# Attention, routing and experts on one core: embedding, gates, ranks and early plan in steps of one slot, the early plan from two batches

## Chip, cores and metric

One core of a Trainium2 chip runs the whole program. The metric is the time of one execution in microseconds (us), the median of three runs for the kernel before. Engines are named as in the profile: PE (TensorE; PEld its weight loads), DVE (VectorE), ACT (ScalarE), POOL (GpSimd) and SP (SyncE, which here issues nearly all loads).

## What is computed

```python
# attention: q, k, v of (4 batches, 12 heads, 448 tokens, 64)
scores = matmul(q, k.T) / sqrt(64) - log(448)
attn_out = matmul(1 / (1 + exp(-scores)), v)
x = attn_out.transpose(0, 2, 1, 3).reshape(1792, 768)

# mixture of 8 experts, one expert per token
xn = x / (norm(x) + 1e-06);  en = emb / (norm(emb) + 1e-06)
logits = xn @ en.T / tau
expert_idx = argmax(logits, axis=1)
gate_w = softmax(logits)[arange, expert_idx]
out[mask_e] = gate_w * (relu(x[mask_e] @ w1[e]) @ w2[e])

# dense layer
h = out @ w_in              # (768, 2048)
y = (h - tanh(h)) @ w_out   # (2048, 768)
```

Every float32 product is made of three products of rounded parts (a high part h, a low part l: hh, hl, lh), so that each operand needs a cast (`w0h`, `vh`, `ah`) and a subtraction (`w0l`, `vl`, `al`).

## The kernel before

**Attention** runs from 0 to about 232 us. Its work is cut into 84 slots; 24 pairs of heads (6 for each of 4 batches) share them, 7 slots for two pairs. In slot u PE makes the scores of slot u (`pq`, line 233), then the products with v of slot u-3 (`pav`, line 256; LAG = 3). Between the two, ACT takes two sigmoids of `pq` (lines 240, 241) and DVE their difference `al` (line 242), which frees the PSUM tile of `pq`. When a pair is done, its columns are copied out (`xT`), and two slots later PE turns them into rows of tokens and logits (`pr`, line 281), which DVE adds to `u` (291) and copies into `rec` (292). For the pairs to come DVE casts `w0h`/`w1h` (199) and `vh` (210), and POOL makes `w0l`/`w1l` (202) and `vl` (211).

The PSUM tiles `pq`, `pr` and `prank` come from one tag, "qk", with three buffers in turn: a tile waits until the tile three allocations earlier has been read. Only PE's order is written out by hand: a loop over slots calls `scores(u)`, `av(u - LAG)` and `events(u)`, which runs what `plan(u, ...)` put down for that slot. The orders of DVE, ACT, POOL and SP are a scheduler's; each of these queues is worked off in that order.

**Routing.** When the last pair of a batch has its rows, `route` finds each token's expert (`route_a`) and plans the rest for fixed slots: the squares for the norm on ACT (`square`), the gate value (`gate`), the ranks of the tokens within their expert (`route_b`: `prank` on PE, then some ten small DVE operations that read it in PSUM, up to the row numbers `idx`) and four scatters of the rows to a table in DRAM, sorted by expert (`send_rows`, POOL, line 491, `x_tok`).

```python
if b == B - 2:
    plan(now[0] + ROUTE_E - 1, self.gate, b, r)      # ROUTE_E = 3
    plan(now[0] + ROUTE_E, self.route_b, b, r, pr)
    plan(now[0] + ROUTE_E, self.send_rows, b, r)
    plan(now[0] + ROUTE_E, self.early_rows)
    plan(ns, self.early_gates)
elif b < B - 1:
    plan(now[0] + ROUTE - 1, self.gate, b, r)        # ROUTE = 8
```

**Early plan.** After the third batch `early_rows` (called B - 2 = 2) chooses, from three batches' counts, the two expert groups of 256 tokens that are worked first (`plan_early`, some 60 small DVE operations named `pe_...`, up to the row numbers `gidx`), loads the first three quarters of the first group's w1 (`w1raw`, SP) and gathers both groups' rows (`gather_x`, POOL, line 698, `xg`). `early_gates` multiplies the first group's rows by their gates on ACT (line 706). So the experts can start at 239 us, while the last batch is routed. **Experts** run to about 560 us (9 groups, PE without pauses), the **dense layer** from there to the end.

Of the kernel before, what the change touches and what calls it, by code (L numbers as in the profile page):

```python
# [23 lines left out]
ROUTE, ROUTE_E = 8, 3  # L24
# [14 lines left out]
class Prog:  # L39
# [56 lines left out]
    def embedding(self):  # L96
        nc, E, NJ = self.nc, self.E, self.NJ
        cp, ep = self.cp, self.ep
        et = cp.tile([P, NJ, E], F32, name="emb_t")
        nc.sync.dma_start(et, self.emb)  # L100
        sq = ep.tile([P, NJ, E], F32, name="emb_sq")
        nc.vector.tensor_tensor(sq, et, et, ALU.mult)
        pt = self.ps1.tile([P, 2, 512], F32, tag="qk", name="emb_ss")[:, 0]
# [4 lines left out]
        self.norm_plus_eps(ss, sc[:, 0], sc[:, 1], self.mhalf[:, 0:1].to_broadcast([P, E]))  # L108
        nc.vector.reciprocal(sc[:, 0], sc[:, 1])
        self.ien = ep.tile([P, NJ, P + E], F32, name="ien")  # L110
        nc.vector.tensor_copy(self.ien[:, :, :P], self.ident.unsqueeze(1).to_broadcast([P, NJ, P]))
        nc.vector.tensor_tensor(
            self.ien[:, :, P:], et, sc[:, 0].unsqueeze(1).to_broadcast([P, NJ, E]), ALU.mult
        )

    def norm_plus_eps(self, ss, tmp, res, mhalf):

        nc = self.nc
        shape = list(ss.shape)
        r0 = self.sm.tile(shape, F32, tag="nr0", name="nr0")  # L120
        nc.vector.tensor_scalar(ss, ss, 1e-30, None, ALU.max)
        nc.gpsimd.tensor_tensor(r0, ss, mhalf, ALU.pow)
        nc.vector.tensor_tensor(tmp, r0, r0, ALU.mult)
        nc.vector.scalar_tensor_tensor(tmp, tmp, -0.5, ss, ALU.mult, ALU.mult)
        nc.vector.scalar_tensor_tensor(tmp, tmp, 1.5, r0, ALU.add, ALU.mult)
        nc.vector.tensor_tensor(tmp, tmp, ss, ALU.mult)
        nc.vector.tensor_scalar(res, tmp, 1e-6, None, ALU.add)


    def attention(self):  # L130
# [206 lines left out]
        with tc.manual_schedule(engines=pe):  # L337
# [10 lines left out]

            def route(i):
                b = pairs[i][0]  # L350
                bt = self.bts.pop(b)
                for c in range(NCH):
                    plan(now[0] + 1 + c // 2 if b < B - 1 else now[0], square, bt, c)
                r = self.route_a(bt)
                pr = lambda: ps1.tile([P, 2, 512], F32, tag="qk", name="prank")
                if b == B - 2:
                    plan(now[0] + ROUTE_E - 1, self.gate, b, r)
                    plan(now[0] + ROUTE_E, self.route_b, b, r, pr)
                    plan(now[0] + ROUTE_E, self.send_rows, b, r)
                    plan(now[0] + ROUTE_E, self.early_rows)  # L360
                    plan(ns, self.early_gates)
                    plan(ns + 1, self.early_columns, lambda: ps2.tile([P, 2, 512], F32, tag="qk", name="xt"))
                elif b < B - 1:
                    plan(now[0] + ROUTE - 1, self.gate, b, r)
                    plan(now[0] + ROUTE, self.route_b, b, r, pr)
                    plan(now[0] + ROUTE, self.send_rows, b, r)
                else:
                    self.last_route = b, r
# [11 lines left out]
            plan(5, self.embedding)  # L380
            now = [0]
            u = 0
            while u < ns + LAG:
                now[0] = u
                if u < ns:
                    scores(u)
                if LAG <= u < ns + LAG:
                    av(u - LAG)
                events(u)
                if u >= CONV:  # L390
                    conv()
                if u == ns and self.cv is not None:
                    for _ in self.cv:
                        pass
                u += 1
        while at:
            now[0] = u
            events(u)
            u += 1
        cx.close()  # L400

    def route_a(self, bt):
# [8 lines left out]
        nc.vector.tensor_reduce(mx, lg, AX.X, ALU.max)  # L411
        ls = sm.tile(A3, F32, tag="ls", name="ls")
# [9 lines left out]
        return bt, oh, ls  # L422

    def route_b(self, b, st, pst):
        bt, oh, ls = st
# [18 lines left out]
        V.tensor_tensor(o, o, cnt, ALU.subtract)  # L444
        rk = sm.tile(A3, F32, tag="rk", name="rk")
# [7 lines left out]
        bt["idx"] = idx  # L453

    def send_rows(self, b, st):

        bt = st[0]
# [9 lines left out]
    def gate(self, b, st):  # L467

        bt, oh, ls = st
        nc, sm = self.nc, self.sm  # L470
# [16 lines left out]
        nc.vector.reciprocal(bt["rec"][:, :, DM + 1 : DM + 2], gs.unsqueeze(2))  # L487

# [33 lines left out]
    def plan_early(self):  # L522
# [4 lines left out]
        cnt0 = self.n_before[:, self.B - 1]  # L527
        pls = []
        self.start = self.n_first = None
        for k in range(2):  # L530
# [11 lines left out]
            V.tensor_scalar(e, cm, -1.0, float(E), ALU.mult, ALU.add)  # L542
            m = t("m", P, 2)
# [9 lines left out]
            nb = self.B - 1  # L553
# [4 lines left out]
            V.tensor_reduce(vs, pr, AX.X, ALU.add)  # L558
            gidx = cp.tile([P, 1, 2], I32, name=f"gidx0{k}")
# [3 lines left out]
            V.tensor_copy(pl["e"], e)  # L563
            st = t("start", P, E)
# [9 lines left out]
            pls.append(pl)  # L574

# [7 lines left out]
        return pls  # L583
# [90 lines left out]
    def early_rows(self):  # L674
        self.pl0, self.pl1 = self.plan_early()
# [4 lines left out]
        nt = (self.B - 1) * self.S  # L680
        for s in (self.s0, self.s1):
            for h in range(2):
                self.gather_x(s, h, nt)
# [74 lines left out]
    def experts(self, cx):  # L758
# [83 lines left out]
        def last_route():  # L842
            self.route_b(*self.last_route, pst)
            self.gate(*self.last_route)
            self.send_rows(*self.last_route)
            pl.update(self.plan())
# [324 lines left out]
```

## Time and profile before

| | |
|---|---|
| median of 3 runs | 1052.88 us (1050.65 to 1053.71) |
| the profiled execution | 1052.65 us, its span 1050.9 us |
| PE busy, DVE busy | 97% and 79% of the span |
| 98.53 to 116.94 us, slots 35 to 41 | 18.41 us |
| 134.61 to 153.78 us, slots 49 to 55 | 19.17 us |
| 153.78 to 172.19 us, slots 56 to 62 | 18.41 us |
| 189.86 to 211.23 us, slots 70 to 76 | 21.37 us |
| 211.23 to 228.30 us, slots 77 to 82 | 17.07 us |

How to read it: a timeline row gives start, length, engine, line, operation and, in brackets, how long the engine stood idle before it and what released it. PE is in front of everything here, so a loss shows as a bracket on a PE row, or as a stretch of seven slots that is longer than a quiet one. What the other engines do counts where PE waits for it. All slot numbers count from 0.

### The profile page before, as it was taken

How to read it: one execution, taken by the hardware profiler on the slowest of the kernel's cores; microseconds unless marked ns; L12 is line 12 of the kernel's file. 1: busy time of each engine (PE TensorE's matmuls, PEld its weight loads, DVE VectorE, ACT ScalarE, POOL GpSimd, SP SyncE). 2: the span in 40 equal slices, each digit the busy share in tenths (PEclk: the TensorE clock that was granted, in tenths of full speed). 3: DMA queues.
4: the chain of work that ended last, by engine and by line, in shares of the span. 5: the costliest groups of instructions: out<-in, count | busy, mean ns of one | idle time of the engine just before them, and what ended most of it. 6: DMA issues, size and time to landing. Idle time of an engine off the chain costs nothing.

```text
span 1050.9 us, 16813 instructions
## 1 busy us (share of the span) xinstructions
PE 1016.5 (97%) x6437; PEld 939.6 (89%) x6437; DVE 828.9 (79%) x1172; ACT 557.0 (53%) x694; POOL 166.4 (16%) x178
## 2 busy tenths in 40 slices
PE   7999999899999999999998999999999999999997
PEld 5777777678999999999997899999999999999997
DVE  7879797978968878889963798888987676766774
ACT  6778787777666666666643544442453322332230
POOL 7345546342021001010000000000000300000002
PEclk9999999999999999999999999999999999999999
DMA  5422424338878984874922535454443522332212
GB/s 160 140 83 82 134 65 142 118 115 299 297 243 299 337 290 162 282 257 161 309 103 94 197 139 175 180 210 150 181 151 120 193 94 89 120 120 98 113 61 106
DMA packets 83527, 175.28 MB, mean 167 GB/s; under 512 B 7639, under 2 KB 62958, under 8 KB 83438
## 3 DMA queue, kind: packets, MB, share of 16 engines
q1 hardware_dynamic: 79598, 155.78, 43.2%
q0 software_dynamic: 3840, 18.35, 4.9%
q8 instruction: 52, 0.85, 0.3%
q14 instruction: 37, 0.30, 0.1%
HBM read 156.68 MB, written 36.30 MB: 184 GB/s over the span
## 4 chain that ended last, share of the span: by engine, by line
issue 57%; PE 29%; DVE 8%; POOL 3%; DMA 2%; ACT 1%; SPq 0%; POOLq 0%; DVEq 0%; ACTq 0%
PE pty L786 8%; PE pth L786 8%; PE pav L256 6%; PE pq L233 4%; POOL out_dram L491 2%; DVE al L242 2%; PE pr L281 1%; DVE vh L210 1%; DMA xg<-x_tok,gidx 1%; DVE wl L777 1%; PE xt L725 1%; DMA cr<-in_moe_w_in_dram 1%; ACT wh L776 1%; POOL vl L211 0%; DVE xT L271 0%
## 5 line engine op out<-in xcount | busy, mean ns | idle before, releaser
L1041 PE MATMUL o<-wo,gh 128*128 128x384 f32 x896 | 240.8, 335 | 0.7 <-DVE acc L1054 0.7
L1001 PE MATMUL z<-yh,wi 128*128 128x448 f32 x768 | 221.2, 370 | 4.1 <-ACT yh L973 3.8
L1041 PEld LDWEIGHTS o<-wo,gh 128*128 128x128 f32 x896 | 163.3, 188 | 2.3 <-DVE acc L1054 1.0
L1001 PEld LDWEIGHTS z<-yh,wi 128*128 128x128 f32 x768 | 144.3, 189 | 16.9 <-ACT yh L973 4.2
L1041 PE MATMUL o<-wo,gl 128*128 128x384 f32 x448 | 150.1, 335 | 0.1
L1001 PE MATMUL z<-yl,wi 128*128 128x448 f32 x384 | 138.0, 367 | 0.0
L786 PE MATMUL pth<-wi,wh 128*128 128x256 f32 x432 | 121.4, 282 | 2.9 <-ACT wi L729 1.2
L1054 DVE TENSOR_TENSOR acc<-o,acc 128x768 f32<-128x768 f32 x97 | 92.4, 952 | 39.5 <-PE o L1041 38.3
L786 PE MATMUL pty<-hh,wl 128*128 128x256 f32 x432 | 121.7, 284 | 0.2 <-DVE wl L777 0.2
L786 PE MATMUL pth<-wi,wl 128*128 128x256 f32 x432 | 121.3, 281 | 0.3 <-DVE wl L777 0.3
L786 PE MATMUL pty<-hh,wh 128*128 128x256 f32 x432 | 121.5, 285 | 0.0
L786 PE MATMUL pty<-hl,wh 128*128 128x256 f32 x432 | 121.3, 283 | 0.0
L786 PE MATMUL pth<-xl,wh 128*128 128x256 f32 x432 | 120.9, 280 | 0.0
L240 ACT ACTIVATE ah<-pq,bias_s 128x896 fp32r<-128x896 f32 x84 | 85.2, 1014 | 45.5 <-PE pq L233 45.5
L242 DVE TENSOR_TENSOR al<-pq,ah 128x896 fp32r<-128x896 f32 x84 | 90.4, 1084 | 23.8 <-ACT pq L241 23.3
L491 POOL DMA_INDIRECT out_dram<-acc,toki x14 | 17.2, 1232 | 577.9 <-DVE acc L1054 576.7
L1024 ACT CAST gh<-r 128x896 fp32r<-128x896 f32 x32 | 30.0, 938 | 135.1 <-DVE r L1022 82.2
L1008 ACT ACTIVATE t<-z 128x896 f32<-128x896 f32 x32 | 29.4, 920 | 127.3 <-PE z L1001 73.8
L777 DVE TENSOR_TENSOR wl<-w1raw,wh 128x768 fp32r<-128x768 f32 x72 | 68.2, 955 | 25.0 <-ACT wh L776 24.3
L1041 PEld LDWEIGHTS o<-wo,gl 128*128 128x128 f32 x448 | 84.1, 188 | 1.7 <-DVE gl L1025 0.4
L786 PEld LDWEIGHTS pth<-wi,wh 128*128 128x128 f32 x432 | 81.6, 189 | 3.5 <-ACT wi L729 1.4
L786 PEld LDWEIGHTS pty<-hh,wl 128*128 128x128 f32 x432 | 82.4, 191 | 0.4 <-DVE wl L777 0.4
(249 smaller groups left out, 2200.4 us busy)
## 6 DMA issues: line engine op xcount, KB each, us to landing
w1raw<-in_moe_w_dram SPq DMA_DIRECT2D x36, 768.0 KB
w2raw<-in_moe_w_dram SPq DMA_DIRECT2D x27, 1024.0 KB
wi<-dwi SPq DMA_DIRECT2D x32, 768.0 KB
wo<-dwo SPq DMA_DIRECT2D x32, 768.0 KB
cr<-in_moe_w_in_dram SPq DMA_DIRECT2D x16, 768.0 KB
dwi<-cr SPq DMA_DIRECT2D x16, 768.0 KB
cr<-in_moe_w_out_dram SPq DMA_DIRECT2D x16, 768.0 KB
dwo<-cr SPq DMA_DIRECT2D x16, 768.0 KB
```

What stands on the lines that cost most here:

```text
L233: nc.tensor.matmul(pq[:, x, :S], w[kt][p, c : c + P], w[qt][p, KW:], start=(m == 0), stop=(m == 2))
L240: nc.scalar.activation(hi, pv, AF.Sigmoid, **sc)
L242: nc.vector.tensor_tensor(lo, pv, f32(hi), ALU.subtract)
L256: nc.tensor.matmul(pav[:, :S], vo(vv), aa[:, x], start=(b0 and m == 0), stop=(e and m == 2))
L491: i = self.nc.gpsimd.indirect_dma_start(**kw)
L777: nc.vector.tensor_tensor(wl, cols, f32(wh), ALU.subtract)
L786: nc.tensor.matmul(pt[:, u], a[:, kk], b[:, kk], start=(n == 0), stop=(n == 3 * K - 1))
L1001: nc.tensor.matmul(z[:, g, :GT], wi[:, a, j * P : (j + 1) * P], b[:, j], start=(n == 0), stop=(n == 3 * NJ - 1),)
L1008: nc.scalar.activation(t, zv, AF.Square)
L1024: nc.scalar.copy(gv, r)
L1041: nc.tensor.matmul(o[:, w, :NW], a[:, u, i * P : (i + 1) * P], wo[:, b, w * NW : (w + 1) * NW], start=(n == 0), stop=(n == 3 * CH - 1),)
L1054: nc.vector.tensor_tensor(acc[i], ov, acc[i], ALU.add)
```

## The change

`embedding`, `route_a`, `norm_plus_eps`, `gate`, `route_b`, `early_rows` and `plan_early` become generators; a list of them is stepped once in each slot, after `events(u)`. The fixed offsets ROUTE and ROUTE_E go. The counts and ranks are copied out of PSUM once (`rks`), and the rank arithmetic reads the copy. For the last batch, routed inside the first expert group, the order of gate and ranks stays. The early plan is made from BE = 2 batches, so right after batch 1's ranks instead of batch 2's, with 3 table products in place of 5. `early_gates` no longer has to be issued after the last sigmoid.

```diff
-ROUTE, ROUTE_E = 8, 3
+BE = 2
...
-    def embedding(self):
+    def embedding(self, pst):
...
         nc.sync.dma_start(et, self.emb)
+        for _ in range(3):
+            yield
...
+            def step():
+                for g in list(tasks):
+                    if next(g, 1) is not None:
+                        tasks.remove(g)
...
             def route(i):
                 b = pairs[i][0]
                 bt = self.bts.pop(b)
...
+                def steps():
+                    yield from self.route_a(bt)
+                    for c in range(NCH):
+                        square(bt, c)
+                        yield
+                    if b == B - 1:
+                        return
+                    yield from self.gate(bt)
+                    yield from self.route_b(b, bt, pr)
+                    self.send_rows(b, bt)
+                    if b == BE - 1:
+                        yield
+                        yield from self.early_rows()
...
+                task(steps())
...
-            plan(5, self.embedding)
+            plan(2, task, self.embedding(pr))
+            plan(ns, self.early_gates)
...
                 events(u)
+                step()
...
     def route_b
...
+        rks = sm.tile([P, NCH + 1, E], F32, tag="rks", name="rks", bufs=1)
+        nc.vector.tensor_copy(rks, pr)
+        yield
-        cnt, V = pr[:, NCH], nc.vector
+        pr, cnt, V = rks, rks[:, NCH], nc.vector
...
     def plan_early
...
-        cnt0 = self.n_before[:, self.B - 1]
+        cnt0 = self.n_before[:, BE]
...
-            nb = self.B - 1
+            nb = BE
...
     def early_gates(self):
-        with self.tc.issue_after(self.last_sig.ins):
-            for h in range(2):
-                self.gate_rows(self.s0, h)
+        for h in range(2):
+            self.gate_rows(self.s0, h)
```

Where the instructions move is seen in the queues' orders. DVE around slot 55, **before** (`prank` of batch 1 is made after slot 54; the first `al` here is slot 54's):

```order
L487 RECIPROCAL yT_last<-gs 112x4
L444 TENSOR_TENSOR ro<-ro,prank 128x8
L242 TENSOR_TENSOR al<-pq,ah 128x896
L446 TENSOR_TENSOR rk<-prank,ro 112x32
L452 SCALAR_TENSOR_TENSOR shift<-ro,n_before 128x8
L199 CAST w1h<-kq_192 128x960
L271 COPY xT<-pav 128x448
L210 CAST vh_202<-vr 128x4x64 x2
L447 TENSOR_TENSOR rk<-rk,oh 112x32
L242 TENSOR_TENSOR al<-pq,ah 128x896
L449 TENSOR_REDUCE rs<-rk 112x4
L451 TENSOR_SCALAR idx<-rs 112x4
```

The rank operations stand around the `al` of slots 54 to 56, three of them between those of slots 54 and 55.

The same place **after the change** (the first `al` is slot 55's; `prank` is made after slot 56 now, and slot 55's `al` follows its copies directly):

```order
L245 TENSOR_TENSOR al<-pq,ah 128x896
L459 COPY rks<-prank 128x40
L464 TENSOR_TENSOR n_before<-n_before,rks 128x8
L467 TENSOR_TENSOR rt<-c_tri,rks 128x64
L564 TENSOR_REDUCE pe_mx_1893<-n_before 128x1
L468 TENSOR_REDUCE ro<-rt 128x8
L245 TENSOR_TENSOR al<-pq,ah 128x896
L566 SCALAR_TENSOR_TENSOR pe_cand_1895<-n_before,pe_mx_1893,w_80 128x8
L573 TENSOR_SCALAR pe_m_1928<-pe_mx_1893 128x1
L469 TENSOR_TENSOR ro<-ro,rks 128x8
L567 TENSOR_REDUCE pe_cm_1896<-pe_cand_1895 128x1
L574 TENSOR_SCALAR pe_m_1928<-pe_m_1928 128x1
```

The ranks stand one and two slots later, and the early plan's `pe_...` operations, which followed batch 2's ranks at slots 70 to 77 before, run on from here to the `al` of slot 61: 52 of them, with the rows of two pairs, three casts and the rest of the ranks in between.

POOL, **before**: batch 1's scatters and what follows them, to the `vl` of pair 18 (`vl_203`; `vl_207` is pair 17's; `w0l` is pair 18's, `w1l` pair 19's).

```order
L491 DMA x_tok<-yT_last,idx 896x784 x4
L211 TENSOR_TENSOR vl_207<-vr,vh_206 128x4x64 x2
L294 COPY yT_last<-tok 112x4
L202 TENSOR_TENSOR w0l<-kq_190,w0h 128x448
L202 TENSOR_TENSOR w0l<-kq_190,w0h 128x512
L202 TENSOR_TENSOR w1l<-kq_191,w1h 128x448
L202 TENSOR_TENSOR w1l<-kq_191,w1h 128x512
L211 TENSOR_TENSOR vl_203<-vr,vh_202 128x4x64 x2
```

POOL **after the change**, over the same stretch:

```order
L519 DMA x_tok<-yT_last,idx 896x784 x4
L214 TENSOR_TENSOR vl_207<-vr,vh_206 128x4x64 x2
L205 TENSOR_TENSOR w0l<-kq_190,w0h 128x448
L205 TENSOR_TENSOR w0l<-kq_190,w0h 128x512
L297 COPY yT_last<-tok 112x4
L731 DMA xg<-x_tok,gidx_1981 128x784 x2
L205 TENSOR_TENSOR w1l<-kq_191,w1h 128x448
L205 TENSOR_TENSOR w1l<-kq_191,w1h 128x512
L731 DMA xg<-x_tok,gidx_2157 128x784 x2
L214 TENSOR_TENSOR vl_203<-vr,vh_202 128x4x64 x2
```

The four gathers stand ahead of `w1l` and of pair 18's `vl`, and the copy into `rec` (here `yT_last`), which waits for the scatters' landing, is behind `w0l` instead of ahead of it.

In ACT's queue the two gatings of the first early group's rows (`xg<-xg`) move from behind the last slot's sigmoids to behind those of slots 63 and 64, **after the change**:

```order
L243 ACTIVATE ah<-pq,bias_s 128x896
L244 ACTIVATE pq<-pq,bias_s 128x2x448
L739 ACTIVATE xg<-xg 128x768
L243 ACTIVATE ah<-pq,bias_s 128x896
L244 ACTIVATE pq<-pq,bias_s 128x2x448
L739 ACTIVATE xg<-xg 128x768
L243 ACTIVATE ah<-pq,bias_s 128x896
L244 ACTIVATE pq<-pq,bias_s 128x2x448
```

Each of them stands ahead of the sigmoids of the next slot. On SP the loads of the first three `w1raw` move from behind all loads of attention to about slot 58, between the loads for pairs 20 and 21, with the reads of the plan's numbers ahead of them.

## Rows read from the trace of the kernel before

**Rows 1.** The page, part 1: busy time (share of the span) and instructions of each engine.

```profile
PE 1016.5 (97%) x6437; PEld 939.6 (89%) x6437; DVE 828.9 (79%) x1172; ACT 557.0 (53%) x694; POOL 166.4 (16%) x178
```

**Rows 2.** Windows: stretch, length; busy PE, PEld, DVE, ACT, POOL; clock, DMA share, GB/s.

```profile
61.76:79.41 17.65, 17.65 (x101) 13.56 (x100) 14.58 (x26) 13.97 (x17) 7.76 (x8) 1.00 0.29 83
...
134.61:153.78 19.17, 17.84 (x108) 13.76 (x107) 18.05 (x38) 16.38 (x25) 8.74 (x9) 1.00 0.26 77
...
153.78:172.19 18.41, 17.98 (x101) 13.46 (x101) 14.65 (x22) 13.61 (x16) 12.19 (x13) 1.00 0.49 144
...
189.86:211.23 21.37, 18.00 (x108) 13.80 (x107) 21.32 (x96) 15.74 (x24) 8.72 (x9) 1.00 0.39 124
...
211.23:228.30 17.07, 15.76 (x89) 11.93 (x88) 13.21 (x25) 12.46 (x15) 10.21 (x12) 1.00 0.27 82
...
199.00:202.00 3.00, 3.00 (x18) 2.51 (x18) 3.00 (x15) 2.71 (x4) 2.45 (x3) 1.00 0.97 324
```

**Rows 3.** Timeline of PE, 149 to 207 us: start, length, line, op, [idle before <-releaser].

```profile
149.20 0.47 PE L233 MATMUL pq<-w1h 64*128 64x448 f32 x2 [1.33 <-DVE al L242]
...
158.66 0.34 PE L281 MATMUL pr<-ien,xT 128*112 128x136 f32 x1 [0.37 <-DVE rs L449]
...
179.72 0.36 PE L233 MATMUL pq<-w0h 128*128 128x448 f32 x1
...
193.76 0.47 PE L233 MATMUL pq<-w0h 64*128 64x448 f32 x2 [1.47 <-DVE n_before L439]
...
206.27 0.48 PE L233 MATMUL pq<-w1h 64*128 64x448 f32 x2 [1.48 <-DVE al L242]
```

**Rows 4.** Timeline of DVE, 154 to 159 us: from the last copies of slot 55 on.

```profile
154.60 2.27 DVE L210 CAST vh<-vr 128x256 fp32r<-128x256 f32 x2
...
156.79 0.72 DVE L447 TENSOR_TENSOR rk<-rk,oh 112x32 f32<-112x32 f32 x1
...
157.44 1.08 DVE L242 TENSOR_TENSOR al<-pq,ah 128x896 fp32r<-128x896 f32 x1
```

**Rows 5.** Timeline of DVE, 193 to 208 us: small operations of ranks and early plan.

```profile
193.53 0.14 DVE L439 TENSOR_TENSOR n_before<-n_before,prank 128x8 f32<-128x8 f32 x1
...
194.91 0.22 DVE L547 TENSOR_SCALAR pe_pos<-c_pos,pe_m 128x2 f32<-128x2 f32 x1
...
200.59 1.27 DVE L594 TENSOR_TENSOR pe_ro<-pe_ro 128x2 f32<-128x2 f32 x1
...
206.21 1.25 DVE L571 TENSOR_TENSOR pe_m<-pe_m,pe_m 128x1 f32<-128x1 f32 x1
```

**Rows 6.** Timeline of POOL, 159 to 206 us.

```profile
159.10 1.02 POOL L491 DMA_INDIRECT x_tok<-yT_last,idx  x1 [0.93 <-DVE idx L451]
...
162.91 0.94 POOL L491 DMA_INDIRECT x_tok<-yT_last,idx  x1 [0.30 <-issue]
...
168.31 0.19 POOL L294 COPY yT_last<-tok 112x4 f32<-112x4 f32 x1 [2.51 <-DMA x_tok<-yT_last,idx]
...
168.46 2.38 POOL L202 TENSOR_TENSOR w0l<-kq,w0h 128x448 fp32r<-128x448 f32 x2
...
205.04 2.40 POOL L202 TENSOR_TENSOR w0l<-kq,w0h 128x448 fp32r<-128x448 f32 x2 [3.19 <-issue]
```

**Rows 7.** The page, part 5: the sigmoid of scores; busy, mean ns, idle before.

```profile
L240 ACT ACTIVATE ah<-pq,bias_s 128x896 fp32r<-128x896 f32 x84 | 85.2, 1014 | 45.5 <-PE pq L233 45.5
```

**Rows 8.** Timeline of ACT, 228 to 236 us: gating of the first early group.

```profile
232.87 0.94 ACT L706 ACTIVATE xg<-xg 128x768 f32<-128x768 f32 x1 [0.85 <-DMA xg<-x_tok,gidx]
```

**Rows 9.** One tile, x_tok: all its scatters and gathers, from issue to landing.

```profile
DMA to landing us min/median/max: 3.5/4.8/8.8
```

**Rows 10.** Timeline of SP, 190 to 200 us: loads of the first weights.

```profile
197.47 1.59 SPq L753 DMA_DIRECT2D w1raw<-in_moe_w_dram  x3
```

**Rows 11.** Timeline of DVE, 18 to 19 us: the embedding.

```profile
18.90 0.21 DVE L102 TENSOR_TENSOR emb_sq<-emb_t 128x48 f32<-128x48 f32 x1 [1.28 <-DMA emb_t<-in_moe_expert_emb_dram]
```

**Rows 12.** Timeline of ACT, 249 to 250 us: gates of the last batch.

```profile
249.59 0.23 ACT L480 ACTIVATE sg<-ls 112x32 f32<-112x32 f32 x1 [2.21 <-DVE ls L478]
```

More of the change, by code (lines that the diff above doesn't have):

```diff
@@ L100, in embedding @@
         nc.sync.dma_start(et, self.emb)
+        for _ in range(3):
+            yield
         sq = ep.tile([P, NJ, E], F32, name="emb_sq")
         nc.vector.tensor_tensor(sq, et, et, ALU.mult)
-        pt = self.ps1.tile([P, 2, 512], F32, tag="qk", name="emb_ss")[:, 0]
+        pt = pst()[:, 0]
         nc.tensor.matmul(pt[:, : NJ * E], self.ones, sq.rearrange("p j e -> p (j e)"), start=True, stop=True)
@@ L107, in embedding @@
         sc = cp.tile([P, 2, E], F32, name="emb_sc")
-        self.norm_plus_eps(ss, sc[:, 0], sc[:, 1], self.mhalf[:, 0:1].to_broadcast([P, E]))
+        yield from self.norm_plus_eps(ss, sc[:, 0], sc[:, 1], self.mhalf[:, 0:1].to_broadcast([P, E]))
         nc.vector.reciprocal(sc[:, 0], sc[:, 1])
@@ L347, in events, with task @@
                 at.pop(u, None)
+            tasks = []
+            def task(g):
+                tasks.append(g)
+            def step():
+                for g in list(tasks):
+                    if next(g, 1) is not None:
+                        tasks.remove(g)
+            pr = lambda: ps1.tile([P, 2, 512], F32, tag="qk", name="prank")
             def route(i):
@@ L351, in route @@
                 bt = self.bts.pop(b)
[L352 to L368, printed above, removed]
+                def steps():
[11 more added lines that the diff above has]
+                        yield from self.early_rows()
+                if b == B - 1:
+                    self.last_route = b, bt
+                task(steps())
             for i in range(n):
@@ L379, in attention @@
                     plan(final[i] + LAG + ROW, route, i)
-            plan(5, self.embedding)
-            now = [0]
+            plan(2, task, self.embedding(pr))
+            plan(ns, self.early_gates)
+            plan(ns + 1, self.early_columns, lambda: ps2.tile([P, 2, 512], F32, tag="qk", name="xt"))
             u = 0
             while u < ns + LAG:
-                now[0] = u
                 if u < ns:
@@ L396, in attention @@
         while at:
-            now[0] = u
             events(u)
             u += 1
+        while tasks:
+            step()
         cx.close()
@@ L465, in send_rows, with gate @@
             )
-    def gate(self, b, st):
-        bt, oh, ls = st
-        nc, sm = self.nc, self.sm
+    def gate(self, bt):
+        nc, sm, ls = self.nc, self.sm, bt["ls"]
         E, DM = self.E, self.DM
@@ L674, in early_rows @@
     def early_rows(self):
-        self.pl0, self.pl1 = self.plan_early()
+        yield from self.plan_early()
+        self.pl0, self.pl1 = self.pls
         self.e0 = self.reg(self.nc.sync, self.pl0["e"], 0, self.E - 1)
@@ L842, in last_route @@
         def last_route():
-            self.route_b(*self.last_route, pst)
-            self.gate(*self.last_route)
-            self.send_rows(*self.last_route)
+            b, bt = self.last_route
+            for _ in self.route_b(b, bt, pst):
+                pass
+            for _ in self.gate(bt):
+                pass
+            self.send_rows(b, bt)
             pl.update(self.plan())
```

32 lines of the change are left out of this document (22 added, 10 removed).

## Prediction

> **What bounds the kernel now.** I read the page's busy line first: PE works 1016.5 of 1050.9 us and DVE 828.9 [rows 1], so a change of other engines' order can pay only where PE stands idle. The windows came next, seven slots at a time. Quiet slots take 17.65 us, all of it PE's, with DVE busy for 14.58 [rows 2]: 2.23 us a slot, and about 1.02 more for each of the two `pr`. Against that, slots 49 to 55 take 1.52 more, slots 56 to 62 0.76 more (batch 0's slots 35 to 41 take the same 18.41, in the table above), slots 70 to 76 3.72 more. Slots 77 to 82 are six, 15.42 when quiet, and take 17.07, so 1.65 more [rows 2]. In slots 70 to 76 DVE is busy for 21.32 of 21.37 us: there, where the early plan meets batch 2's gate, DVE is the bound.
>
> Then PE's timeline, for what the waits are. In slot 54 `pq` waits 1.33 us for an `al`; around the early plan `pq` waits 1.47 for `n_before` (in fact for the `prank` tile to be read) and 1.48 for an `al` [rows 3]. All are waits for a PSUM buffer of the tag "qk": the tile three allocations earlier has not been read yet, since DVE is late.
>
> DVE's timeline says why it is late. 16 small operations run from 193.53 to 195.04, 0.092 us apart [rows 5]. But some take 1.25 us and more, and these end with POOL's work: the one at 206.21 ends at 207.46, POOL's `w0l` at 207.44 [rows 5, 6]. The casts of `vh`, too, take 2.27 us for two [rows 4]. So a small operation costs 0.09 us, or up to 1.27 where POOL is at work on `w0l`, `w1l` or `vl`.
>
> **The change, part by part.** The sum is made against the profiled execution, 1052.65 us, 0.23 below the median of 1052.88.
>
> *Ranks of batches 0 and 1, two slots later.* `prank` leaves slot 54, 0.2 us less on PE there (the rest of that stretch's 1.52 is the 1.33, which nothing touches). In slot 56 it takes a buffer, so that `pq` of slot 57 now needs the tile of slot 55, three allocations back, hence that slot's `al`. Before, this `al` ran from 157.44 to 158.52, behind `vh` (to 156.87) and a rank operation of 0.72 [rows 4]; now it follows `vh` and should end at about 157.7. `pq` of slot 57 was due at 153.78 + 2.23 = 156.0, so it loses about 1.8; the later loss of this stretch, 0.76 with `pr`'s 0.37 [rows 2, 3], mostly goes. Net +0.8 for each batch, bounds 0 (the wait overlaps with what is lost today) and +1.0. The copy `rks` adds one small operation per batch, in DVE's idle time of these slots (18.41 less 14.65).
>
> *The early plan, from slots 70 to 77 to slots 56 to 61.* 52 operations at 0.092 are 4.8 us of DVE, and `rks` and the ranks moved in some 0.6 more. DVE's 14.65 of slots 56 to 62 [rows 2] becomes 20.1, over the 18.41 that the stretch takes now, and that without a long operation; two of 1.25 us beside `w0l` [rows 5] make 22.3. Bounds: the plan hides in full and only the rank term is left, +0.8, or DVE sets the pace with both long ones, 22.3 - 18.41 = +3.9. I take +3.0 for the stretch, ranks included, near the upper end, since the nearest row is the same plan in slots 70 to 76, where DVE did become the bound. Less 0.2 for slots 49 to 55.
>
> *Slots 70 to 82.* Without the plan they should look like batch 1 without it: 1.3 lost in slots 70 to 76 instead of 3.72, and 0.76 + 0.8 instead of 1.65 in slots 77 to 82. That gives back 2.5, which I take; bounds 2.1 (ranks at 1.0 and the 0.2 of `prank` not saved) and 3.1 (batch 1's 1.52 + 0.76 as they are now).
>
> *Gathers on POOL, gatings on ACT.* `idx` now stands behind the `al` of slot 57 and a pair's rows. From 157.7: five operations 0.5, `al` 1.0, 17 operations 1.6, `al` 1.0, rows and `idx` 0.8 give 162.6, and POOL scatters from 163.1, 4.0 later than 159.10 [rows 6]. The scatters land 9.2 after the first (159.10 to 168.31 [rows 6]), at 172.3; the first gather is issued at 172.5 and lands 4.8 later [rows 9], at 177.3. ACT wants it behind slot 63's sigmoids: the slot begins where the stretch ends, at 172.19 [rows 2], some 3.0 late by then, and 0.8 of scores and two sigmoids of 1.0 [rows 7] make 178.0. With `rec`'s copy and the hops 178.4 at the latest. So it is just hidden. If it isn't, ACT stands, with slot 64's sigmoids behind it: gating 0.94 [rows 8], two sigmoids 2.0, `al` 1.1 and the hops, 4.3 us in all, and then `pq` of slot 66, whose buffer is the tile of slot 64 (`pq`, `pr`, `pq` in between), due at 179.72 [rows 3] and 3.0 late, 182.7. So each microsecond that the first gather lands after 178.4 is lost. POOL's `vl` of pair 18, behind both pairs of gathers, has some 2 us to spare by the same reckoning. Against it stand the three `w1raw` loads, which filled the DMA engines for a while (share 0.97, 324 GB/s [rows 2]) after 197.47 [rows 10], when no scatter ran; now they are issued at about 162.5, with the scatters. The landings range from 3.5 to 8.8 us [rows 9]: scatters and gather each at the slow end would be 4.0 later, and `pq` 2.9 to 6.9 later. Bounds 0 and +6.9; I take 2 us of delay, so +0.9.
>
> On this place the Trainium skill speaks ("DMA: Bandwidth & Descriptors", section "Queues, rings and completion order"): each DMA engine takes turns between the queues that have work, packet by packet. By that the scatters are neither ahead of the weights nor behind all of them, which fits a delay between my two bounds; no run here shows the two together.
>
> *At nothing.* The embedding: its load goes out three slots earlier, so that DVE's wait of 1.28 [rows 11] goes, but PE's matmul stays where it was in PE's order, so nothing on PE starts sooner. Gatings no longer behind the last sigmoid: ACT's wait of 0.85 there [rows 8] ends before PE, which has transposes to do, needs the columns. SP's reads and loads ahead of those of pair 21: two pairs are loaded ahead. *The last batch's gate* comes a little earlier in DVE's queue, and ACT waits 2.21 for it [rows 12]: -0.3, between 0 and -0.6.
>
> Sum: +0.8 - 0.2 + 3.0 - 2.5 + 0.9 - 0.3 = **+1.7**. The median becomes 1052.88 + 1.7 = **1054.6 us**.
>
> **Rivals.** *The plan hides, faster.* DVE has 3.8 us idle in slots 56 to 62 and 3.1 in the seven after them [rows 2], and plan operations have no one waiting for them; if the long ones stay away, the terms are 0 for batch 0, -0.2, 0 for the stretch, -3.1, 0 and -0.3: -3.6, 1049.3. For it speaks that slots 56 to 62 have no gate chain; against it the long operations and that PE follows DVE by three buffers at most.
>
> *Weights against scatters, slower.* One mechanism: `w1raw` beside the scatters delays the landing, ACT stands at the first gating ahead of slot 64's sigmoids, and PE at `pq` of slot 66. Without the gathers the sum is +0.8. A delay of one slow landing, 4.0, makes it +0.8 + 2.9 = +3.7, 1056.6; of two +7.7, 1060.6. It decides for slower from a landing 3.5 us late. The 8.8 in the trace speaks for it; against it, that the loads are over after some 7 us.
>
> *The issue itself blocked, slower.* An issue by POOL could have to wait for a copy that DVE has begun, as DVE's casts wait for POOL's work: up to 2.27 / 2 = 1.1 us each [rows 4]. Four gathers would hold `vl` back by 4.5 us, less the 2 to spare: +2.5 on my sum, 1057.1. Against it: the scatters take 0.94 to 1.02 us each with DVE at work beside them [rows 6]. The chance is 0.03. The Trainium skill has this rule ("SBUF — State Buffer", section "SBUF: two separate sides"): float32 copies on DVE lock GpSimd out of a shared port, and it cannot write descriptors until they end. The trace shows the lock on DVE's operations beside POOL's, but on no issue.
>
> *The change only moves the wait:* what is lost at 56 to 61 is what is gained at 70 to 77, 0 in sum. That is within my forecast's range.
>
> **How the numbers follow.** About 0.3%, 3.2 us, is what a measurement of this kernel can tell from no change. The forecast's case has 0.57, the hidden plan 0.18, weights against scatters 0.20, blocked issues 0.03, 0.02 is left for what I don't see. The hidden plan passes the 3.2 us mostly: faster 0.15. Of the forecast's case, some 0.07 lies above +3.2; with the two others slower 0.30. Same 0.55. The range: all lower ends together (ranks 0, stretch +0.8, landings 0, -3.1, -0.6, and the -0.2) make -3.1, and the hidden plan -3.6; I set 1050.0, which leaves some of that case out. Above, one slow landing and a half, 6.0 late, makes +0.8 + 4.9 = 5.7, and 1059.0 takes in the rank terms' upper ends.
>
> **What would show it.** Right: `pq` of slot 57 (and 36, 78) waiting over 1 us for an `al`; slots 56 to 62 over 20.5 us with DVE busy nearly throughout; slots 70 to 76 near 19; the first gating on ACT with little wait. Wrong: slots 56 to 62 near 18.4 (the plan hidden), slots 70 to 76 still over 20, or a wait of several us on ACT for the gathered rows with PE idle at slot 66.

## The result, and the profile after

The change takes **1057.38 us** (median of 6 runs, 1056.46 to 1059.89). The kernel before took 1051.53 beside it on the same chip (6 runs, 1050.51 to 1053.71; the 1052.88 above is the median of three of these). The ratio is 1.0056, 95% interval 1.004 to 1.0072: **slower by 5.85 us**. Its profiled execution took 1058.36, with a span of 1056.7 against 1050.9, so the two traces show the difference in full (5.8).

Windows of the change, for the stretches that [rows 2] and the text behind it compare (stretch, length; busy PE, PEld, DVE, ACT, POOL; clock, DMA share, GB/s), from slots 28 to 34 to slots 77 to 82, without the quiet slots 42 to 48:

```profile
79.22:98.20 18.98, 17.70 (x102) 13.56 (x101) 17.79 (x33) 16.38 (x25) 8.70 (x9) 1.00 0.29 77
98.20:117.54 19.34, 17.84 (x106) 13.79 (x105) 14.81 (x30) 13.60 (x16) 11.84 (x13) 1.00 0.50 147
135.20:154.59 19.39, 17.68 (x103) 13.56 (x102) 17.93 (x33) 16.38 (x25) 8.75 (x9) 1.00 0.27 76
154.59:176.83 22.24, 18.27 (x107) 13.93 (x106) 22.04 (x81) 14.00 (x16) 12.24 (x14) 0.98 0.71 232
176.83:195.53 18.70, 18.70 (x101) 14.30 (x100) 13.12 (x25) 15.22 (x19) 11.07 (x12) 0.93 0.57 169
195.53:214.62 19.09, 17.75 (x102) 13.57 (x102) 17.93 (x33) 16.40 (x25) 8.76 (x9) 1.00 0.06 14
214.62:231.67 17.05, 15.59 (x94) 12.25 (x93) 12.55 (x26) 11.71 (x14) 9.13 (x10) 1.00 0.27 83
```

Against before, stretch by stretch: slots 35 to 41 +0.93 (19.34 less 18.41), 49 to 55 +0.22, 56 to 62 **+3.83**, 63 to 69 +1.03 (18.70 less 17.67), 70 to 76 **-2.28**, 77 to 82 -0.02; what lies ahead of slot 35 adds -0.3. (42 to 48 are unchanged.) So attention ends 3.4 later. The rest, 2.4, comes behind it: from the first product of the experts (`pth`) to the first of the dense layer (`z`) 331.0 us where it was 329.5, and from there to the end 483.3 where it was 482.4.

**Slots 56 to 62** have DVE busy for 22.04 of 22.24 us. PE's timeline of the change, its waits there, with the slot after them:

```profile
158.50 0.47 PE L236 MATMUL pq<-w0h 64*128 64x448 f32 x2 [1.50 <-DVE rks L459]
...
174.21 0.47 PE L236 MATMUL pq<-w1h 64*128 64x448 f32 x2 [2.48 <-DVE al L245]
...
176.83 0.74 PE L236 MATMUL pq<-w0h 64*128 64x448 f32 x2
```

DVE's and POOL's timelines say what the 2.48 is. DVE, then POOL:

```profile
169.35 0.14 DVE L594 CAST pe_eo<-pe_e 128x1 int32<-128x1 f32 x1
169.41 2.91 DVE L597 TENSOR_SCALAR pe_start<-pe_oh,pe_m 128x8 f32<-128x8 f32 x1
172.23 0.15 DVE L601 TENSOR_TENSOR pe_new<-pe_e,pe_e 128x1 int32<-128x1 f32 x1
...
173.07 1.08 DVE L245 TENSOR_TENSOR al<-pq,ah 128x896 fp32r<-128x896 f32 x1
```

```profile
167.56 0.94 POOL L519 DMA_INDIRECT x_tok<-yT_last,idx  x1 [0.31 <-DMA w1raw<-in_moe_w_dram]
168.53 1.42 POOL L214 TENSOR_TENSOR vl<-vr,vh 128x256 fp32r<-128x256 f32 x2
169.92 2.37 POOL L205 TENSOR_TENSOR w0l<-kq,w0h 128x448 fp32r<-128x448 f32 x2
...
175.56 0.19 POOL L297 COPY yT_last<-tok 112x4 f32<-112x4 f32 x1 [3.27 <-DMA x_tok<-yT_last,idx]
176.28 1.02 POOL L731 DMA_INDIRECT xg<-x_tok,gidx  x1 [0.54 <-issue]
```

An operation on 8 elements a partition takes 2.91 us and ends at 172.32, 0.03 behind the end of POOL's `w0l` (172.29). The `al` behind it, which PE's `pq` needs, starts at 173.07. POOL's four scatters had held `vl` and `w0l` back until they stood back to back, in the middle of the plan. The rows of before have locks of 1.27 at most [rows 5]; this one is more than twice as long.

**Slots 62 and 63** then run at half clock. Windows of two microseconds of the change (columns as above):

```profile
172.00:174.00 2.00, 0.00 (x0) 0.00 (x0) 2.00 (x11) 0.30 (x1) 0.28 (x1) 1.00 1.01 391
174.00:176.00 2.00, 1.79 (x11) 1.39 (x12) 1.97 (x10) 0.82 (x1) 0.19 (x1) 0.97 1.08 350
176.00:178.00 2.00, 2.00 (x9) 1.11 (x7) 2.00 (x5) 1.06 (x2) 1.41 (x2) 0.50 0.53 116
178.00:180.00 2.00, 2.00 (x8) 1.46 (x6) 1.13 (x2) 1.58 (x2) 1.99 (x3) 0.68 0.87 247
```

PE stood still for the whole of the first row, ran, and from about 176 its granted clock was 0.50, that is 1.2 of 2.4 GHz. The pair of `pq` at 176.83 takes 0.74 instead of 0.47. That is the 1.03 of slots 63 to 69 (all 18.70 us of them PE's) and some 0.4 of slot 62.

**The gathers** make nobody wait, but only just. The scatters start at 163.69 and have landed at 175.56, 11.9 later (9.2 before, [rows 6]). The first gather is issued at 176.28, and no gather of this trace lands in less than 3.7 us, so its rows were there at about 180 at the earliest. ACT's first gating starts at 180.36, without idle time behind slot 63's sigmoids:

```profile
180.36 0.94 ACT L739 ACTIVATE xg<-xg 128x768 f32<-128x768 f32 x1
```

**Behind attention** PE runs the same products a little slower. From the page's part 5, the experts' first product before and after (busy us, mean ns of one, idle before):

```profile
L786 PE MATMUL pth<-wi,wh 128*128 128x256 f32 x432 | 121.4, 282 | 2.9 <-ACT wi L729 1.2
```

```profile
L819 PE MATMUL pth<-wi,wh 128*128 128x256 f32 x432 | 122.6, 285 | 1.9 <-ACT wi L762 1.1
```

It waits less and each takes 1% longer. From the start of one product to that of the next (about 1900 steps below 0.2 us between 300 and 545 us, mean) it is 0.1193 us before and 0.1206 after, all at clock 1.00. Nothing in the change touches these products. The second product, `pty`, is no slower, before and after:

```profile
L786 PE MATMUL pty<-hh,wh 128*128 128x256 f32 x432 | 121.5, 285 | 0.0
```

```profile
L819 PE MATMUL pty<-hh,wh 128*128 128x256 f32 x432 | 121.1, 285 | 0.0
```

Taken apart, the steps of `pth` grow from 0.1179 to 0.1199 us and those of `pty` stay at 0.1197 and 0.1198. There are 3 x 432 of `pth`, which makes 2.6 us.

### The profile page after: what moved, and what is told of

It reads as the page before. It is cut to its first block, busy times and chain, and to the rows that moved or that the text cites. A ratio compares the mean times of both kernels' runs of the same rounds, so it can differ in the third digit from the quotient of the medians.

```text
span 1056.7 us, 16795 instructions
## 1 busy us (share of the span) xinstructions
PE 1019.9 (97%) x6437; PEld 943.7 (89%) x6437; DVE 830.9 (79%) x1164; ACT 558.4 (53%) x694; POOL 159.9 (15%) x178
## 4 chain that ended last, share of the span: by engine, by line
issue 57%; PE 31%; DVE 5%; POOL 3%; ACT 2%; DMA 1%; POOLq 0%; SPq 0%; DVEq 0%; ACTq 0%
PE pth L819 9%; PE pty L819 8%; PE pav L259 7%; PE pq L236 5%; POOL out_dram L519 2%; PE pr L284 1%; DVE al L245 1%; DVE vh L213 1%; DMA xg<-x_tok,gidx 1%; PE xt L758 1%; DMA cr<-in_moe_w_in_dram 1%; ACT ah L243 1%; ACT wh L809 0%; ACT pq L244 0%; POOL vl L214 0%
## 5 line engine op out<-in xcount | busy, mean ns | idle before, releaser
L810 DVE TENSOR_TENSOR wl<-w2raw,wh 128x1024 fp32r<-128x1024 f32 x54 | 65.9, 1221 | 30.1 <-ACT wh L809 30.1
```

The lines of the kernel that those rows point to most:

```text
L810: nc.vector.tensor_tensor(wl, cols, f32(wh), ALU.subtract)
```

## Experiments

**e0, the kernel before, again**, unchanged, for the spread between two executions.

> The kernel before, unchanged, for a second profile. In the profiles at hand the stretch from the first product of the experts to the first of the dense layer takes 328.7 us before and 330.2 after the change, and the rest 482.4 and 483.3. If these 2.4 us are scatter from run to run, the stretch differs from 328.7 here by 0.5 or more; if the change makes them (the first two groups are experts 2 and 4 instead of 4 and 2), it is 328.7 within 0.3.

Measured: 1050.64, span 1048.9. Its start is 2.6 us quicker (slot 14 at 41.47, before at 44.11), the experts take 329.5 from their first product on, as before (the 328.7 above leaves out the first products), with 0.1193 us a product. So the pace of the products repeats; the start of attention doesn't: from 30 to 60 us the granted clock is 1.00 here and 0.94 in the profile of before. In the change's profile it is 0.94 too, so the comparison above is not touched by it.

**e1, the move alone**: in the kernel before, the early plan is made after two batches, in the old slots of the ranks, without steps.

```diff
-                if b == B - 2:
-                    plan(now[0] + ROUTE_E - 1, self.gate, b, r)
...
+                if b == 1:
+                    plan(now[0] + ROUTE - 1, self.gate, b, r)
...
-            nb = self.B - 1
+            nb = 2
...
```

> The kernel before with the early plan made from two batches, after batch 1's ranks, and nothing in steps: ranks of batches 0 and 1 at their old slots, read in PSUM. Theory 1 (the later ranks cost 0.9 in each batch, and one plan operation is locked for 2.9 us by POOL's w0l; the place of the plan as such costs little): slots 35 to 41 as before, 18.4; slots 70 to 76 near 19.1; slots 56 to 62 between 18.5 and 20.5, by what stands beside POOL's work; 1050 to 1053 us. Rival (DVE has no room in slots 56 to 62 for the plan, however it is cut): slots 56 to 62 over 21.5, 1055 us or more. If the order of the experts costs 1.5 us, it shows here too.

Measured: 1053.9 (10 runs, 1052.21 to 1057.4), ratio 1.0024 (1.0011 to 1.0037). Slots 56 to 62 take 22.61, slots 70 to 76 19.18, slots 77 to 82 16.10. PE, DVE and POOL:

```profile
157.34 1.15 PE L281 MATMUL pr<-ien,xT 128*112 128x136 f32 x8 [1.44 <-DVE al L242]
...
169.53 0.47 PE L233 MATMUL pq<-w1h 64*128 64x448 f32 x2 [2.89 <-DVE al L242]
```

```profile
165.28 3.00 DVE L552 TENSOR_SCALAR pe_pos<-pe_pos,pe_so 128x2 f32<-128x2 f32 x1
```

```profile
164.04 1.91 POOL L211 TENSOR_TENSOR vl<-vr,vh 128x256 fp32r<-128x256 f32 x2
165.91 2.34 POOL L202 TENSOR_TENSOR w0l<-kq,w0h 128x448 fp32r<-128x448 f32 x2
```

It is the same lock, of another operation of the plan, over `vl` and `w0l` together. So the lock belongs to the move and not to the steps, and the move alone costs 2.5 of the 5.9 us (1.2 to 3.9 by the interval). The clock did not fall behind this wait of 2.89 (1.00 from 170 to 174), and a product of the experts takes 0.1194 us.

**e2, ranks two slots later still**: two empty steps between gate and ranks.

```diff
                     yield from self.gate(bt)
+                    yield
+                    yield
                     yield from self.route_b(b, bt, pr)
```

> The change with two more empty steps ahead of the ranks: prank is made in slots 37, 58 and 79, where the tile three allocations earlier than the next scores is that of the rows (pr), which has been read. Theory 1: the waits of 1.5 us for rks at the scores after prank go, 0.9 to 1.5 us in each of three batches, so slots 35 to 41 near 18.2 and the whole 2.5 to 4 us faster than the change, if the plan, two slots later, is not locked worse. Rival (the waits are DVE's lateness and only turn up at another slot): slots 35 to 41 stay at 19.3, no gain.

Measured: 1063.35 (4 runs), ratio 1.0102 (1.0076 to 1.0129). Slots 35 to 41 still take 19.34, slots 56 to 62 19.66, but 63 to 69 23.31 and 70 to 76 19.81:

```profile
172.49 0.47 PE L236 MATMUL pq<-w1h 64*128 64x448 f32 x2 [1.74 <-DVE al L245]
...
183.97 2.13 PE L284 MATMUL pr<-ien,xT 128*112 128x136 f32 x8 [2.50 <-DVE pe_ro L626]
```

The waits turn up at other slots, as the rival had it: the plan, two slots later, meets POOL's work there. The `pr` of 2.13 instead of 1.15 us is again at half clock.

**e3, the plan pinned**: each step of the early plan stands behind the `al` of its own slot in DVE's queue, one step a slot.

```diff
-                        yield from self.early_rows()
+                        yield from pinned(self.early_rows())
...
+            def pinned(g):
+                while True:
+                    with tc.issue_after(self.last_al.ins):
+                        r = next(g, 1)
```

> The change with each step of the early plan held behind the al of its slot on DVE, so that it takes slots 61 to 71 and not 56 to 61. Theory 1 (one operation locked beside w0l made pq of slot 62 wait 2.48 us, and the halved clock after it cost 1.5): slots 56 to 62 near 19.5 instead of 22.24, no granted clock below 1.0 in slots 62 and 63, slots 63 to 69 at 17.7 to 19; 2 to 4 us faster than the change. Rival (the plan's 5 us of DVE work cost PE the same wherever they stand): what slots 56 to 62 give back, slots 63 to 76 lose.

Measured: 1056.48 (6 runs), ratio 1.0038 (1.0025 to 1.005), against 1.0056. Slots 56 to 62 take 19.34 and 63 to 69 17.79: the wait of 2.48 and the half clock there are gone. But the plan now lasts until batch 2's gate, and slots 70 to 76 take 20.32:

```profile
198.99 1.15 PE L284 MATMUL pr<-ien,xT 128*112 128x136 f32 x8 [2.14 <-DVE al L245]
```

In this execution the clock fell at slot 36 instead, behind the wait of 1.50 for `rks`. By medians pinning gives some 1.9 us net (1.0056 - 1.0038), but the two intervals overlap, so that the gain is not shown.

**e4, the change 32 bytes lower.** `rks` needs 160 bytes of SBUF a partition, and every tile behind it moves. The plan's tables, made for two batches, give 128 back ahead of the experts' tiles, so that their `wh` moves from 68288, a multiple of 64 bytes, to 68320, 32 above one. Here one small tile loses its second buffer, and `wh` starts at 68288 again; the order of all engines is that of the change.

```diff
-        o = sm.tile([P, E], F32, tag="ro", name="ro")
+        o = sm.tile([P, E], F32, tag="ro", name="ro", bufs=1)
```

> The change with one buffer fewer for a 32-byte tile (ro), so that every tile behind it starts 32 bytes lower per partition; no instruction moves on any engine. In the five profiles so far the experts' products follow each other every 0.1193 us in the kernels without the copy rks and every 0.1206 in those with it; rks (160 bytes, the plan's tables 128 fewer) moves the tiles of the experts from addresses that are multiples of 64 to 32 above one. Theory (the address costs PE 1%): 0.1193 here, experts and dense layer 2 to 3.5 us shorter, 1054 to 1055.5 us. Rival (something else in the change, such as the other order of the experts): 0.1206, and 1057.4 as the change.

**e5, the kernel before 160 bytes higher**: an unused tile of the size of `rks` (`wh` at 68448, again a multiple of 64 plus 32), and its one memset on POOL.

```diff
+        nc.gpsimd.memset(self.sm.tile([P, NCH + 1, self.E], F32, tag="rks", name="rks", bufs=1), 0.0)
```

> The kernel before with an unused tile of 160 bytes per partition in the place of rks and one more memset on POOL, nothing else. Theory (the address costs PE 1%): products every 0.1206 us, 2 to 3.5 us slower than before, 1054 to 1056. Rival: 0.1193, as before, 1051.5 to 1052.5.

Measured: e4 1055.94 (12 runs, 1051.65 to 1059.88), ratio 1.0024 (1.0011 to 1.0038); e5 1055.91 (12 runs), ratio 1.0033 (1.0023 to 1.0043). The page's row of the experts' first product, e4 and then e5:

```profile
L819 PE MATMUL pth<-wi,wh 128*128 128x256 f32 x432 | 121.5, 282 | 2.0 <-ACT wi L762 1.1
```

```profile
L787 PE MATMUL pth<-wi,wh 128*128 128x256 f32 x432 | 122.9, 285 | 2.8 <-ACT wi L730 1.2
```

The 32 bytes decide it, both ways: 0.1193 us a product in e4 and 0.1201 in e5, and 328.5 and 331.6 us for the experts (the change 331.0, before 329.5). The kernel before with nothing but another address and one memset is 0.33% slower; the change with the old address is 0.32% quicker (1.0056 - 1.0024). That is about 3.4 us by medians; the traces show 2.5 (e4) and 2.1 (e5) of it in the experts. The dense layer does not follow the address: from its first product to the end it takes 484.0 us in e4, more than the change's 483.3. e4's median is a little above what the theory gave it.

By medians e4 costs just what the move alone costs (e1, 1.0024 too), so these runs show no price of the steps and the later ranks beside it. The spread of e4 is wide, and it goes with the clock: over the whole execution the granted clock was 0.997 in its quickest run and 0.987 in the two slowest. Its profiled execution has the clock fall at four places from slot 36 on, behind each of the waits at slots 36, 57 and 78 for `rks` among them. Windows of e4 behind slot 36's (columns as above):

```profile
100.00:103.00 3.00, 2.08 (x11) 1.68 (x12) 2.89 (x10) 1.11 (x2) 1.04 (x2) 0.90 0.64 175
103.00:106.00 3.00, 3.00 (x15) 2.59 (x15) 1.79 (x5) 0.77 (x1) 1.97 (x2) 0.54 0.33 99
```

**e6, the move pinned**: e1 with the plan cut into steps, one a slot from slot 57, each behind its slot's `al`; the ranks as before, no `rks`.

```diff
-                    plan(now[0] + ROUTE, self.early_rows)
+                    g = self.early_rows()
+                    for k in range(14):
+                        plan(now[0] + ROUTE + 2 + k, pinned, g)
...
```

> e1 with the plan in steps, each held behind the al of its slot on DVE, slots 57 to 67; the ranks stay where they are before the change, and no rks. If the long waits of e1 (1.44 at pr of slot 57, 2.89 at pq of slot 61) come from operations locked beside POOL's w0l and vl, they go: slots 56 to 62 at 18.4 to 19.5 instead of 22.6, slots 63 to 69 17.7 to 18.5, slots 70 to 82 as in e1 (35.3), so that attention is 2 to 3.5 us shorter than before and the whole 1048.5 to 1050.5. Rival (the plan's DVE work costs PE wherever it stands): slots 56 to 69 together over 39, no faster than before.

Measured: 1052.79 (12 runs, 1050.8 to 1056.32), ratio 1.0011 (0.9999 to 1.0024), not to be told from before. Slots 56 to 62 take what they took before (from 151.39 to 169.82, 18.43), but the lock comes in slots 63 to 69, which take 20.45 and not the 17.7 to 18.5 hoped for; PE, DVE and POOL:

```profile
188.04 0.47 PE L233 MATMUL pq<-w1h 64*128 64x448 f32 x2 [1.17 <-DVE al L242]
```

```profile
183.95 2.25 DVE L590 TENSOR_TENSOR pe_ord<-c_tri,pe_oh 128x64 f32<-128x64 f32 x1
```

```profile
183.73 2.38 POOL L202 TENSOR_TENSOR w0l<-kq,w0h 128x448 fp32r<-128x448 f32 x2
```

**e7, the weights late**, meant to take the `w1raw` loads away from the scatters.

```diff
-        for c in range(NWE):
-            self.weight(self.e0, None, c)
...
+            plan(ns - 7, self.early_weights)
```

> The change with the three w1raw loads issued from slot 77 on instead of slot 58, so that they don't run beside batch 1's scatters. If they held the scatters up (11.9 us from the first one to the copy behind the last one's landing, 9.2 before), it is 9.2 to 9.8 here. In time: my rival (weights against scatters make PE wait) expects 1 to 3 us less; the trace of the change, where ACT and PE did not wait for the gathers, less than 0.5.

Measured: 1059.23 (4 runs), ratio 1.0061 (1.0039 to 1.0082). It missed its aim: SP still issued the loads at 160.01. So it is a second profile of the change: slots 56 to 62 at 23.38, `pq` of slot 62 waiting 2.46 with the clock halved behind it, 0.1205 us a product. What it was to tell, the other runs tell without it: scatters whose landing is over ahead of `w1raw`'s issue take 8.7 us (e6, 156.73 to 165.38) and 9.0 (e3), and those beside it 11.9 (the change, and e7) and 12.0 (e1, to the gather's issue). PE waits for them in none.

**e8, the ranks two slots earlier**: `prank` back in slots 33, 54 and 75, beside the last steps of the gate, and the plan earlier with it.

```diff
-                    yield from self.gate(bt)
-                    yield from self.route_b(b, bt, pr)
+                    g, r = self.gate(bt), self.route_b(b, bt, pr)
+                    next(g)
+                    yield
+                    next(g)
+                    yield
+                    next(g), next(r)
+                    yield
+                    next(g), next(r)
+                    yield
+                    yield from r
```

> The change, but with the ranks of batches 0 and 1 taken two slots earlier (prank in slots 33 and 54, as in the kernel before, batch 2's in slot 75), and the early plan following two slots earlier too. Theory (prank's place costs the wait of 1.5 us at the pq two slots on, since it takes a buffer of the scores where DVE is late): the waits for rks at slots 36, 57 and 78 go; slots 35 to 41 take 18.4 +/- 0.3 us instead of 19.3, slots 77 to 82 about 16.2 instead of 17.05, and slots 49 to 62 together 39 to 41 instead of 41.6 (the plan can still meet POOL's w0l or vl and lock for up to 3 us, in other slots). Products of the experts still at 0.1205 us each, since the tiles lie as in the change. Median 2 to 4 us below the change: 1053.5 to 1055.5, ratio to the kernel before 1.002 to 1.004. Rival (these waits only turn up at another slot, as they did with the ranks two slots later): 1056.5 to 1060, ratio 1.005 or more, slots 28 to 41 together still 38 us or more.

**e9, all three at once**: e8, with the plan pinned as in e3 and the 32 bytes of e4.

> All three causes taken away at once: ranks two slots earlier as in the run before, each step of the early plan behind the al of its slot, and the 32 bytes taken off so that the tiles of the experts start at a multiple of 64 bytes as in the kernel before. Theory: the causes add up, so nothing is left of the 5.9 us but what the slots 56 to 69 lose to the plan (about 1), against the 2.2 that slots 70 to 76 gain: 1049.5 to 1052.0, ratio 0.998 to 1.0005; products of the experts at 0.1195 us; no wait over 1.5 us in slots 56 to 62. Rival (plan's work only moves, DVE is late somewhere whatever its order): 1053 to 1056, ratio over 1.001, with a wait of 2 us or more in slots 56 to 69.

Measured: e8 1059.92 (5 runs), ratio 1.0061 (1.0047 to 1.0075); e9 1053.6 (11 runs, 1051.24 to 1056.28), ratio 1.0006 (0.9996 to 1.0016).

In e8 the waits for `rks` are gone, yet slots 35 to 41 take 19.16, since the `pr` there now waits 0.99 for a rank operation, and slots 56 to 62 take 25.54. PE, DVE and a window behind them (columns as above):

```profile
171.76 0.74 PE L236 MATMUL pq<-w1h 64*128 64x448 f32 x2 [3.06 <-DVE al L245]
```

```profile
167.52 3.06 DVE L621 TENSOR_TENSOR pe_ordd<-pe_ord,pe_oh 128x64 f32<-128x64 f32 x1
```

```profile
172.00:174.00 2.00, 2.00 (x8) 1.37 (x9) 1.93 (x8) 0.65 (x1) 0.44 (x1) 0.50 1.09 377
```

For e8 the rival's numbers came true, not my theory's. But it does not settle what the ranks' place is worth. e9 has the same order of DVE around slot 36, and there slots 35 to 41 take 18.57, within what the theory gave; one rank operation on 8 elements a partition makes the difference, e8 and then e9:

```profile
100.74 0.75 DVE L486 SCALAR_TENSOR_TENSOR shift<-ro,n_before 128x8 f32<-128x8 f32 x1
```

```profile
101.08 0.15 DVE L494 SCALAR_TENSOR_TENSOR shift<-ro,n_before 128x8 f32<-128x8 f32 x1
```

The same operation in the same place is locked in one execution and not in the other. In e9 the slots 56 to 69 lose 1.6 against before (19.17 and 18.54, no wait over 1.0), a little more than expected; but the plan, at one step a slot, ends beside batch 2's gate, and what slots 70 to 76 should have given is lost in slot 71:

```profile
197.33 1.15 PE L284 MATMUL pr<-ien,xT 128*112 128x136 f32 x8 [1.83 <-DVE pe_ordd L630]
```

The clock then halves (0.50 from 200 to 202) and the stretch takes 22.63. The products are back at 0.1194 us. By medians the causes add up: pinning gave 0.0018, the address 0.0032, the ranks' place nothing, and 1.0056 less both is 1.0006, which is what e9 measures. With intervals of 0.001 to 0.0016 either way, so close an agreement is luck. Some 5 of the 5.9 us are given back, but e9's time is in the rival's range (1053 to 1056) and not in the theory's, and neither e6 nor e9 is quicker than the kernel before.

## Why the prediction was right, and where it was not

The direction and the range held, but 1057.38 is nearer to the upper end than to the forecast: +1.7 was expected on the median, +5.85 came on the runs side by side. The likeliest outcome by its own chances, no change beyond 3.2 us, did not come; slower had 0.30. And that the range held is partly luck: its upper end was made of late gathers, up to +4.9, which cost nothing, and most of what filled it instead had no term. Term by term:

- **Ranks of batch 0, +0.8:** +0.93. `pq` of slot 57 (and 36, 78) waits 1.46 to 1.50 us, where I had 1.8. The `al` that I named runs from 157.27 to 158.35 behind `vh`, and `rks`, which the trace names, ends 0.1 behind it, so the mechanism is as put. What another slot would cost stays open: with the ranks two slots earlier the stretch takes 19.16 in e8 and 18.57 in e9.
- **Slots 49 to 55, -0.2:** +0.22. The wait for an `al` in slot 54 grew from 1.33 [rows 3] to 1.71. Wrong in sign, small.
- **Slots 56 to 62, +3.0:** +3.83, and "DVE sets the pace", the upper bound with 3.9, is what happened: 22.04 of 22.24 us busy. The size of one lock was off: I took 1.25 us for each of two from [rows 5], and it was one of 2.91, while POOL's `vl` and `w0l` ran back to back.
- **Slots 70 to 82, -2.5:** -2.30 (19.09 and 17.05), well inside the bounds.
- **Gathers, +0.9:** 0. The delay of "2 us" was right (11.9 instead of 9.2 for the scatters, 2.7 late), and my reckoning of 163.1 for the first scatter too (163.69). What failed is the last link: I had ACT ready for the first gating at 178.0, and it got there only at 180.36, itself late by the 2.48 wait and the halved clock, when the rows had just landed. So this delay is hidden behind the other loss; without that one the gathers could have cost PE time.
- **The last batch's gate, -0.3:** -0.2 (`pth` waits 0.78 for `ls`, before 0.97).
- **"At nothing":** the embedding and the gatings are at nothing, as put.

Two things have no term. The first is the clock behind a long wait: half speed in slots 62 and 63, 1.0 + 0.4 us. The second is **the step that failed**: "The copy `rks` adds one small operation per batch, in DVE's idle time". As an operation it costs no more than the 0.1 us by which it ends behind the `al`. As a tile it moves the experts' tiles to 32 bytes above a multiple of 64, and that costs about 3.4 us by the medians of e4 and e5, 2.1 to 2.5 in the experts by their traces. With both, the two traces' sum is 0.93 + 0.22 + 3.83 + 1.03 (slots 63 to 69, the clock) - 2.30 - 0.3 (ahead of slot 35) + 2.4 (behind attention: 1.5 in the experts, the gate's gain included, and 0.9 in the dense layer, whose cause no run shows) = +5.8.

Of the rivals, *the plan hides* fell with DVE at 22.04 us. *Weights against scatters* was right in its first half and never came to cost PE anything, though its time, 1056.6 to 1060.6, holds the measured one: a right number for a wrong cause. *The issue blocked* fell for the change, whose scatters and gathers of this stretch are issued in 0.94 to 1.02 us as before. But one issue each took 1.29 to 1.49 us in e3, e4, e6 and e8, each time beside a cast of DVE; in e6, POOL and DVE:

```profile
169.40 1.44 POOL L710 DMA_INDIRECT xg<-x_tok,gidx  x1 [0.31 <-issue]
```

```profile
169.35 0.65 DVE L199 CAST w1h<-kq 128x960 fp32r<-128x960 f32 x1
```

So an issue can be held up, by some 0.3 to 0.5 us and not the 1.1 that I put into this rival. *Only moves the wait* is the best account of where PE waits in attention: in e2, e3, e6, e8 and e9 alike the wait turns up wherever the plan goes, between 1.2 and 3.1 us at a time. Its sum of 0 is not what the change shows, with attention 3.4 us longer.

## What to carry to other kernels

Work that was moved into an engine's idle time was paid here by its longest lock, not by its mean: before moving small DVE operations, look at where POOL's elementwise work will stand beside them, its DMA issues included, since these push that work together. A new tile, however small, moves the addresses of all tiles behind it; compare the mean time of each untouched product in both traces before crediting or blaming the edit. One kernel can lose and win for reasons that have nothing to do with each other, so undo each by itself, and add up.

## What the runs showed of the hardware that I had not expected

- **TensorE's pace depends on where its tiles start.** With the experts' `wh` at a multiple of 64 bytes a product of 256 columns followed the last at 0.1193 to 0.1194 us (before, e0, e1, e4, e6, e9), with it 32 bytes above at 0.1201 to 0.1208 (the change, e2, e3, e5, e7, e8). All of it is in the experts' first product: a `pth` followed the last at 0.1178 to 0.1179 us in the first six and at 0.1197 to 0.1199 in the others, a `pty` at 0.1197 to 0.1199 in all twelve profiles, although its tiles moved with the others. So a multiple of 64 as such is not what makes it. In the programs as built one tile of `pth` never moves, the high part of the tokens (`wi`, at 223200, 32 above a multiple of 64 in every kernel). `pth` was quicker where its weights lay otherwise to the 64 bytes than this tile, and as slow as `pty` where both lay alike, as `pty`'s tiles do in every kernel. That fits all twelve profiles, but no run moves one tile alone, so it is not shown.
- **A DVE operation on 2 to 64 elements a partition took up to 3.06 us** where POOL ran `vl` and `w0l` back to back, and ended with `w0l`, within 0.1 us (2.91 in the change, 3.00 in e1, 3.06 in e8). The same operation in the same order took 0.75 us in e8 and 0.15 in e9, so one trace does not tell which operations are locked.
- **The granted clock fell to 0.50, 1.2 of 2.4 GHz, for some 3 to 7 us behind some waits of PE and not behind others:** behind 2.48 (the change), 3.06 (e8), 1.83 (e9) and even 1.50 (e3, e4), but not behind 2.89 (e1), 2.14 (e3), the 1.50 of the change or the 1.47 and 1.48 of before. The Trainium skill ("TensorE: Matmul & The Clock Gate", section "HAM oscillation — how this bites in real kernels") tells of a kernel whose waits between groups of matmuls make the clock drop and come back, and that the price of it is paid each time. The trace of the change agrees, with 0.74 instead of 0.47 us for a pair of `pq`. What decides between the executions stays open, and it is much of the spread: e4's runs reach from 1051.65 us at a mean granted clock of 0.997 to 1059.88 at 0.987. e5's loss is not of this kind: in its profile the clock goes as in that of before, 0.94 from 30 to 60 us and 1.00 in the rest of attention.
